# Column tiles for the scores and the state products of a linear-attention and mixture-of-experts kernel, with re-chosen priorities

## The chip, the cores and the metric

The kernel runs on one core of a Trainium2 chip. The metric is the device time of one execution in microseconds (us). The core has a matrix engine (TensorE: PE in the rows for matmuls, PEld for its weight loads), a vector engine (VectorE, DVE), a scalar engine (ScalarE, ACT), GpSimd (POOL) and a queue engine (SP), and 16 DMA engines that move data between main memory and the on-chip memories. Every engine works through its own instructions in the order in which the program lists them.

## The reference

Three layers follow each other. The first is a linear attention with a complex decay, over 4 batches, 8 heads, 768 steps and a head size of 48:

```python
for t in range(S):
    ar, ai = a_re_n[:, :, t, :, None], a_im_n[:, :, t, :, None]   # normalised to a length of at most 0.999
    new_re = ar * S_re - ai * S_im
    new_im = ar * S_im + ai * S_re
    kv = np.einsum('bhd,bhe->bhde', k[:, :, t], v[:, :, t])
    S_re, S_im = (new_re + kv, new_im)
    y[:, :, t] = np.einsum('bhd,bhde->bhe', q[:, :, t], S_re)
```

The second layer is dense: `h = x @ w_in`, `g = max(h, 0) + alpha * min(h, 0)`, `x = g @ w_out`, with 3072 tokens, 384 features and 2048 hidden units. The third sends each token whose skip score is positive to one of 8 experts (the largest gate logit), each with 384 x 1024 and 1024 x 384 weights, and adds the gated result to the token.

## The kernel before

**Attention in chunks.** The 768 steps are cut into 6 chunks of 128 steps, and chunk and batch together give 24 steps `s`. For each `s`, `elementwise(s)` (labels `E0` to `E23`) turns the decays into running products and phases on ScalarE and VectorE and writes scaled queries `qh` and keys `kh`, 96 rows (real and imaginary part) by 8 heads by 128 steps. `attention(s)` (labels `P0` to `P23`) then does, on TensorE:

- scores (parts `a` and `b`, one for each group of 4 heads): for each head a product of `kh` and `qh` into the PSUM tile `at`, 128 by 128, key steps in the rows and query steps in the columns. One VectorE instruction multiplies all four by a triangular mask into the tile `A`.
- transposed keys: 4 transposes into another `at`, then one ScalarE copy into `kT`. The last chunk, s = 20 to 23, has none, and no state product either.
- outputs (part `y`): `columns(ops)` lists small products with 32 columns of weights each, so that four of them stand side by side in the 128 columns of the array. 16 use the values `vt` as weights and `A` as moving data; from the second chunk on 16 more use the state `St` and `qh`.
- state (part `s`): for each head one product of `kT` (96 columns of weights) and `vt` (48 moving columns) into `sps`, then VectorE updates `St`.

A float32 product is two weight loads and two matmuls in the trace.

**Dense layer.** `moe_block(m)` (labels `M0` to `M11`) takes 256 tokens, that is, two steps `s`. Each value is split into a high and a low part, so each product is three matmuls: into `h` with 256 moving columns, into `acc` with 394. The weights are decoded at the beginning from 64-bit words (labels `d0` to `d15`).

**Experts.** From about 556 us on, `start_of(n)` reads the place of each of 9 items into SP's registers, `gather` fetches an item's tokens by an indirect DMA into `xg`, `load_weights` fetches its weights, and `item` does its products and scatters the result. `gates_of` computes the gate from `xg` on VectorE.

**Order.** The order of all instructions on all engines is made ahead by a planner (`Plan`). Each operation has an engine, an estimated cost, what it depends on, and a priority. The planner plays these costs through and takes, on each engine, the ready operation with the lowest priority number; the order that comes out is the program. Priorities are made from the step number plus a table of single corrections, `SHIFT`, by label and part. For a DMA `lag` and `late` give the time that it takes. What the planner assumes only shapes the order; on the chip an engine waits for what its next instruction really needs.

```python
def start_of(n):                                        # in the planner 0.2 us on SP
    return pl.add("SP", 0.2, read, [plan], [])
pl.add("POOL", 1.1, go, [ids], [xg[:, t, :]], lag=0.7, late=1.0)   # a gather
pl.add("PE", 0.3 + 0.0575 * len(ops), go, ...)          # columns(ops)
```

While the weights are decoded (27 to 55 us in the plan) the planner puts extra matmuls where TensorE would idle.

The line numbers in the profile are those of helpers: L462 is every plain matmul, L467 a transpose, L731 the products of `columns`, L431 a two-tensor operation on VectorE, L439 a scalar-tensor-tensor operation, L424 a ScalarE copy, L419 an activation, L1002 and L1003 the register loads of `start_of`, L1046 the fetch of an item's list, L1056 a gather, L1014 an expert's weights.

Of the kernel before, what the change touches and what calls it, by code (L numbers as in the profile page):

```python
# [11 lines left out]
F32 = mybir.dt.float32  # L12
# [386 lines left out]
def moe_kernel(tc, a, qk, v, w_in, w_out, alpha, w_gs, w1, w2, nat, nat_v, out):  # L399
# [53 lines left out]
    def mm(o, l, r, start, stop):  # L453
        n = cols(o)
        dt = l.dtype
        if dt == F32R:
            cost = max(n, 256) / 2.4 + 13.5
        elif dt == BF16:
            cost = 30
        else:  # L460
            cost = 2 * (max(n, math.prod(l.shape[1:])) / 1.2 + (6 if n <= 128 else 0))
# [31 lines left out]
    with ctx:  # L493
# [12 lines left out]
        mask = cp.tile([128, 128], BF16, name="mask")  # L506
        nc.gpsimd.memset(mask, 1.0)
        nc.gpsimd.affine_select(out=mask, in_=mask, pattern=[[1, 128]], compare_op=ALU.is_ge,
                                fill=0.0, base=0, channel_multiplier=-1)
# [60 lines left out]
        for x in qhs:  # L570
            nc.gpsimd.memset(x.ap()[96:128, :, :], 0.0)
        dec = ExitStack()
# [93 lines left out]
        def attention(s, pri):  # L666
# [12 lines left out]
            m4 = mask.rearrange("p (o f) -> p o f", o=1).to_broadcast([128, 4, 128])  # L679
            As, kTs = [], []  # L680
            for g in range(2):
                pl.pri, pl.part = pri(g), 'ab'[g]
                at = pbuf(at_ps, [128, 512], "at", bufs=2)
                for x in range(4):
                    mm(at[:, x * 128:(x + 1) * 128], kh[:, 4 * g + x, 0:128], qh[0:96, 4 * g + x, :], True, True)
                A = pl.buf(pp, [128, 4, 128], F32, "A", bufs=2)
                tt(A, at.rearrange("p (x t) -> p x t", x=4), m4, ALU.mult)
                As.append(A)
                if not last:
# [4 lines left out]
                    copy(kT, at[:, 0:384].rearrange("p (x d) -> p x d", x=4))  # L694
# [11 lines left out]
            columns(ops)  # L706
            pl.pri, pl.part = pri(3), 's'
            if not last:
                sps = pbuf(s_ps, [128, H * D], "sps")[0:96, :]
                for h in range(H):  # L710
                    mm(sps[:, h * D:h * D + D], kTs[h // 4][:, h % 4, :], vt[:, h * 64:h * 64 + D], True, True)
# [12 lines left out]
            tt(xlo[:, :, cs], y, xhi[:, :, cs], ALU.subtract)  # L724
            pl.part = ''

        def columns(ops):

            def go():
                for n, (o, l, r) in enumerate(ops):  # L730
# [821 lines left out]
```

## Time and profile before

| | us |
|---|---|
| median of 3 runs | 762.5 (762.09 to 762.78) |
| the profiled execution, its own time | 760.46 |
| its span, first to last instruction | 758.3 |
| TensorE busy in the span | 718.6 |
| VectorE busy | 602.1 |
| ScalarE busy | 486.7 |

The times are read as device time of one execution. The span is what the trace covers; the profiled execution's time is 2.2 us longer than its span and 2.0 us under the median. Busy time of TensorE is the union of modelled durations that overlap, so it tells where the engine stood still and not how much work there was; the work is better read from start to start.

### The profile page before, as it was taken

Reading aid. Unit: us, or ns where it says so; the run is one execution under the profiler, and the core shown is the slowest. Engines: PE = TensorE matmul, PEld = TensorE weight load, DVE = VectorE, ACT = ScalarE, POOL = GpSimd, SP = SyncE. Lnnn points to the kernel's source line nnn. Section 1 sums busy time; section 2 is a strip of 40 time slices with the busy share of each in tenths; the row PEclk is TensorE's granted clock in tenths of the full one; section 3 lists DMA queues with packets and bytes.
Section 4 is the critical chain, followed back from the end, with each engine's and each line's share of the span. In section 5 each row is a group of like instructions: output and inputs, shape, how many; then the busy total and the mean of one; then the engine's idle time right before and its main releaser. Section 6 shows DMA issues by size and latency. Waiting matters only on the chain.

```text
span 758.3 us, 16570 instructions
## 1 busy us (share of the span) xinstructions
PE 718.6 (95%) x6372; PEld 695.5 (92%) x6372; DVE 602.1 (79%) x1425; ACT 486.7 (64%) x833; POOL 98.6 (13%) x154
## 2 busy tenths in 40 slices
PE   1789999999999999999999999999997999999996
PEld 0678999999999999999999999999997999999996
DVE  5999999989889899999899898945555635697623
ACT  8969659869779679897948958522325332556411
POOL 4000000111101220011130010101011013710111
PEclk9999999999999999999999999999999999999999
DMA  7595862483744767668475564936215301899500
GB/s 267 161 273 199 239 214 79 124 257 102 189 117 143 188 175 231 183 181 268 137 195 178 180 193 120 250 108 172 87 44 189 126 1 46 274 390 393 181 11 18
DMA packets 84678, 130.53 MB, mean 172 GB/s; under 512 B 8822, under 2 KB 60096, under 8 KB 84592
## 3 DMA queue, kind: packets, MB, share of 16 engines
q1 hardware_dynamic: 79152, 111.19, 48.4%
q0 software_dynamic: 5440, 18.21, 7.6%
q8 instruction: 52, 0.85, 0.5%
q14 instruction: 34, 0.28, 0.1%
HBM read 99.46 MB, written 31.29 MB: 172 GB/s over the span
## 4 chain that ended last, share of the span: by engine, by line
PE 49%; issue 10%; DVE 7%; ACT 5%; DMA 5%; SPq 2%; POOL 1%; POOLq 0%; ACTq 0%; DVEq 0%
PE h L462 20%; PE acc L462 19%; PE at L462 3%; PE y L731 3%; PE sps L462 2%; ACT X L419 2%; ACT L391 2%; DVE X L431 1%; DMA r<-in_w 1%; DMA qh<-qd 1%; PE at L467 1%; DMA lst<-tok,ix 1%; DMA X<-in_qk 1%; DMA kd<-QP 1%; ACT hs L424 1%
## 5 line engine op out<-in xcount | busy, mean ns | idle before, releaser
L462 PE MATMUL h<-xlo,wih 128*128 128x256 f32 x576 | 163.8, 285 | 0.2 <-DVE xlo L431 0.2
L462 PE MATMUL h<-xhi,wih 128*128 128x256 f32 x576 | 162.9, 289 | 0.7 <-ACT hs L424 0.4
L462 PE MATMUL h<-xhi,wil 128*128 128x256 f32 x576 | 163.0, 284 | 0.0
L462 PE MATMUL acc<-woh,gh 128*128 128x394 f32 x384 | 134.4, 350 | 0.2 <-ACT gh L424 0.2
L462 PE MATMUL acc<-woh,gl 128*128 128x394 f32 x384 | 130.4, 347 | 4.2 <-DVE gl L431 4.2
L462 PE MATMUL acc<-wol,gh 128*128 128x394 f32 x384 | 132.1, 344 | 0.0
L419 ACT ACTIVATE X<-X 128x384 f32<-128x384 f32 (+1 forms) x216 | 117.2, 559 | 20.9 <-DVE X L450 7.0
L462 PEld LDWEIGHTS h<-xhi,wih 128*128 128x128 f32 x576 | 108.6, 190 | 3.1 <-ACT hs L424 1.3
L462 PEld LDWEIGHTS h<-xlo,wih 128*128 128x128 f32 x576 | 109.7, 191 | 0.7 <-DVE xlo L431 0.4
L462 PEld LDWEIGHTS h<-xhi,wil 128*128 128x128 f32 x576 | 109.7, 191 | 0.4 <-issue 0.4
L439 DVE SCALAR_TENSOR_TENSOR hs<-hs,alp 128x256 f32<-128x256 f32 x192 | 83.8, 477 | 28.6 <-ACT hs L424 28.1
L424 ACT COPY hs<-h 128x512 f32<-128x512 f32 x96 | 53.7, 583 | 63.0 <-PE h L462 60.7
L391 ACT ACT_TABLE_LOAD x71 | 91.1, 1283 | 1.1
L424 ACT CAST gh<-hs 128x512 fp32r<-128x512 f32 x96 | 58.4, 616 | 47.7 <-DVE hs L439 25.0
L431 DVE TENSOR_TENSOR gl<-hs,gh 128x512 fp32r<-128x512 f32 x96 | 65.2, 685 | 14.8 <-ACT gh L424 14.6
L462 PEld LDWEIGHTS acc<-woh,gl 128*128 128x128 f32 x384 | 71.6, 190 | 5.8 <-DVE gl L431 4.7
L911 POOL DMA_INDIRECT lst<-tok,ix x24 | 36.2, 1510 | 312.1 <-DVE ix L435 261.5
L431 DVE TENSOR_TENSOR X<-X 128x768 f32<-128x768 f32 (+1 forms) x96 | 71.6, 749 | 5.8 <-ACT X L419 5.6
L462 PEld LDWEIGHTS acc<-woh,gh 128*128 128x128 f32 x384 | 72.9, 190 | 1.5 <-ACT gh L424 0.6
L462 PEld LDWEIGHTS acc<-wol,gh 128*128 128x128 f32 x384 | 73.1, 190 | 0.3 <-issue 0.2
L462 PE MATMUL at<-qh,kh 96*128 96x128 f32 x384 | 52.6, 278 | 1.0 <-DMA qh<-qd 1.0
L439 DVE SCALAR_TENSOR_TENSOR X<-X 128x384 f32<-128x384 f32 x96 | 52.1, 549 | 0.9 <-ACT X L419 0.6
(189 smaller groups left out, 1381.1 us busy)
## 6 DMA issues: line engine op xcount, KB each, us to landing
r<-in_w SPq DMA_DIRECT2D x24, 512.0 KB, 7.2
r<-in_w SPq DMA_DIRECT2D x32, 384.0 KB, 8.9
kd<-QP SPq DMA_DIRECT2D x24, 387.0 KB, 4.9
kh<-kd SPq DMA_DIRECT2D x24, 387.0 KB, 4.7
qd<-X SPq DMA_DIRECT2D x24, 384.0 KB, 4.0
qh<-qd SPq DMA_DIRECT2D x24, 384.0 KB, 4.5
X<-in_a POOLq DMA_DIRECT2D x18, 384.0 KB, 5.6
X<-in_qk POOLq DMA_DIRECT2D x18, 384.0 KB, 6.1
```

What stands on the lines that cost most here:

```text
L391: nc.scalar.preload_act_table_set(o)
L419: lambda: nc.scalar.activation(real(o), real(i), f, **{k: real(x) for k, x in kw.items()}),
L424: lambda: nc.scalar.copy(real(o), real(i)), [i], [o])
L431: dve(o, cols(o), lambda: nc.vector.tensor_tensor(out=real(o), in0=real(x), in1=real(y), op=op), [x, y], late=late)
L439: dve(o, cols(o), lambda: nc.vector.scalar_tensor_tensor(out=real(o), in0=real(x), scalar=real(s), in1=real(y), op0=op0, op1=op1), [x, y, s])
L462: pl.add("PE", cost / 1e3, lambda: nc.tensor.matmul(real(o), lhsT=real(l), rhs=real(r), start=start, stop=stop, skip_group_check=True), [l ...
L467: pl.add("PE", 0.09 if cols(o) <= 96 else 0.12, lambda: nc.tensor.transpose(real(o), real(i), ident), [i], [o])
L731: ins = nc.tensor.matmul(real(o), lhsT=real(l), rhs=real(r), start=n < 4, stop=n >= len(ops) - 4, skip_group_check=True)
L911: r = nc.gpsimd.indirect_dma_start(out=lst, out_offset=bass.IndirectOffsetOnAxis(ap=real(ix[:, t:t + 1].bitcast(U32)), axis=0), in_=toks[t ...
```

## The change

The scores of a head become two column tiles of 64 rows. The first has the first 64 key steps as weights and all 128 query steps as moving data; the second has the last 64 key steps and only the last 64 query steps, since the quarter with later keys and earlier queries is masked to zero anyway. For odd heads the two halves of the key steps change places in the array, so that each half of the array has as many columns to stream. `A` is now one of two fixed tiles, cleared once at the start, and the mask is applied by three VectorE instructions in place of one: one of 256 columns on 128 rows, two of 128 columns on 64 rows. Since the key steps of odd heads are swapped, the copy into `kT` becomes three ScalarE copies (even heads; odd heads, each half of the rows to the other half), and the values are swapped in the same way on the host.

The state product of a head becomes three column tiles of 32 weight columns, all heads in one call of `columns`. `columns` has two new arguments: whether each product stands alone, and the planner's cost.

Every entry of `SHIFT` is new. Some costs in the planner change: a matmul of more than 256 columns 2.5 ns more, the two register loads of `start_of` 1.0 us in place of 0.2, the landing of a gather 1 us later. On GpSimd the old mask goes and two masks and two cleared tiles come at the start.

```diff
 SHIFT = {
-    "E0e": 1.5, "E1e": 5.5, "E2e": 3, "E2k": 3.5, "E2x": 2, "E3e": 1.6, "E3k": 4, "E4e": 5.1, "E4q": 2.7,
...
+    "E0k": -60.1, "E2e": -8.5, "E2q": -5.6, "E3e": -16.4, "E3q": -0.5, "E4e": -6.3, "E4q": -8.2, "E5e": -7,
...
-            cost = max(n, 256) / 2.4 + 13.5
+            cost = max(n, 256) / 2.4 + (13.5 if n <= 256 else 16)
...
-        mask = cp.tile([128, 128], BF16, name="mask")
...
+        near = cp.tile([128, 2, 64], BF16, name="near")
...
+        late = cp.tile([128, 4, 64], BF16, name="late")
...
+        A2 = [keep(sp, [128, 4, 128], F32, f"A{n}") for n in range(2)]
+        for x in A2:
+            nc.gpsimd.memset(x.ap(), 0.0)
...
                 at = pbuf(at_ps, [128, 512], "at", bufs=2)
+                ops = []
                 for x in range(4):
-                    mm(at[:, x * 128:(x + 1) * 128], kh[:, 4 * g + x, 0:128], qh[0:96, 4 * g + x, :], True, True)
-                A = pl.buf(pp, [128, 4, 128], F32, "A", bufs=2)
-                tt(A, at.rearrange("p (x t) -> p x t", x=4), m4, ALU.mult)
+                    qx, kx = qh[0:96, 4 * g + x, :], kh[:, 4 * g + x, :]
+                    lo, hi = (0, 64) if x % 2 == 0 else (64, 0)
+                    ops.append((at[lo:lo + 64, x * 128:(x + 1) * 128], kx[:, 0:64], qx))
+                    ops.append((at[hi:hi + 64, x * 128 + 64:(x + 1) * 128], kx[:, 64:128], qx[:, 64:128]))
+                columns(ops, True, 0.1 + 4 * 0.17)
+                A = A2[g]
+                at4 = at.rearrange("p (x t) -> p x t", x=4)
+                tt(A[:, :, 64:128], at4[:, :, 64:128], late, ALU.mult)
+                for half in range(2):
+                    ps = slice(64 * half, 64 * half + 64)
+                    tt(A[ps, half:4:2, 0:64], at4[ps, half:4:2, 0:64], near[ps, half, :].rearrange("p (o t) -> p o t", o=1).to_broadcast([64, 2, 64]), ALU.mult)
...
-                    copy(kT, at[:, 0:384].rearrange("p (x d) -> p x d", x=4))
+                    a4 = at[:, 0:384].rearrange("p (x d) -> p x d", x=4)
+                    copy(kT[:, 0:4:2, :], a4[:, 0:4:2, :])
+                    copy(kT[64:128, 1:4:2, :], a4[0:64, 1:4:2, :])
+                    copy(kT[0:64, 1:4:2, :], a4[64:128, 1:4:2, :])
...
-            columns(ops)
+            columns(ops, False, 0.3 + 0.0575 * len(ops))
...
-                for h in range(H):
-                    mm(sps[:, h * D:h * D + D], kTs[h // 4][:, h % 4, :], vt[:, h * 64:h * 64 + D], True, True)
+                columns([(sps[j:j + 32, h * D:h * D + D], kTs[h // 4][:, h % 4, j:j + 32], vt[:, h * 64:h * 64 + D])
+                         for h in range(H) for j in (0, 32, 64)], True, 0.3 + H * 0.09)
...
-            return pl.add("SP", 0.2, read, [plan], [])
+            return pl.add("SP", 1.0, read, [plan], [])
...
-                pl.add("POOL", 1.1, go, [ids], [xg[:, t, :]], lag=0.7, late=1.0)
+                pl.add("POOL", 1.1, go, [ids], [xg[:, t, :]], lag=0.7, late=2.0)
...
+    vv[:, :, 1::2] = np.roll(vv[:, :, 1::2], 64, axis=1)
```

## Rows read from the trace of the kernel before

**Rows 1.** The page: span, and busy time of each engine.

```profile
span 758.3 us, 16570 instructions
PE 718.6 (95%) x6372; PEld 695.5 (92%) x6372; DVE 602.1 (79%) x1425; ACT 486.7 (64%) x833; POOL 98.6 (13%) x154
```

**Rows 2.** Waits of TensorE: engine, line, releaser; us in total, times, longest.

```profile
PE at L467 <- DVE Ao L439: 19.8, 3, 15.4
```

**Rows 3.** Windows: length, busy PE, PEld, DVE, ACT, POOL, clock, DMA share, GB/s.

```profile
75.00:550.00 475.00, 472.53 (x4474) 458.51 (x4474) 419.21 (x995) 340.69 (x583) 49.70 (x54) 1.00 0.60 173
...
275.00:300.00 25.00, 25.00 (x235) 24.75 (x236) 24.98 (x54) 20.10 (x35) 5.03 (x4) 1.00 0.79 229
```

**Rows 4.** Timeline of TensorE's matmuls from 300 us: start, us, instructions merged.

```profile
300.15 1.05 PE L462 MATMUL at<-qh,kh 96*128 96x128 f32 x8
301.04 0.49 PE L467 MATMUL at<-ident,kh 96*128 96x96 f32 x4
301.37 0.80 PE L462 MATMUL sps<-vt,kT 128*96 128x48 f32 x8
301.99 0.48 PE L462 MATMUL h<-xhi,wih 128*128 128x256 f32 x2
302.31 0.28 PE L462 MATMUL h<-xlo,wih 128*128 128x256 f32 x1
302.43 0.28 PE L462 MATMUL h<-xhi,wil 128*128 128x256 f32 x1
```

**Rows 5.** The same timeline around one step's outputs, from 556 us.

```profile
556.67 0.28 PE L462 MATMUL h<-xhi,wil 128*128 128x256 f32 x1
556.88 1.08 PE L731 MATMUL y<-qh,St 128*32 128x128 f32 x32
557.77 1.06 PE L731 MATMUL y<-A,vt 128*32 128x128 f32 x32
558.76 0.39 PE L462 MATMUL h<-xhi,wih 128*128 128x256 f32 x1
558.99 0.28 PE L462 MATMUL h<-xlo,wih 128*128 128x256 f32 x1
```

**Rows 6.** Tiles sps and y: durations min/median/max in ns, first and last start.

```profile
L462 PEld LDWEIGHTS sps<-vt,kT x320: 159/165/166, 42.2 to 484.0; 128*96 128x96 f32 x160
...
L731 PEld LDWEIGHTS y<-A,vt x768: 106/110/110, 44.6 to 558.5; 128*32 128x32 f32 x192
```

**Rows 7.** Windows, tile y alone: instructions under way in a tenth of a microsecond.

```profile
304.42:304.53 0.11, 0.10 (x4) 0.10 (x8) 0.00 (x0) 0.00 (x0) 1.00 1.16 223
```

**Rows 8.** Groups by line and shape on DVE and ACT: busy us, mean ns.

```profile
L431 DVE TENSOR_TENSOR A<-at,mask 128x512 f32<-128x512 f32 x48 | 32.7, 683 | 5.1 <-PE at L462 4.1 <-PE y L731 0.7
...
L431 DVE TENSOR_TENSOR xlo<-y,xhi 128x384 fp32r<-128x384 f32 x24 | 13.2, 551 | 3.4 <-ACT xhi L424 3.3
...
L424 ACT COPY kT<-at 128x384 f32<-128x384 f32 x40 | 18.9, 473 | 10.7 <-PE at L467 10.7
```

**Rows 9.** Timelines of VectorE from 307 us.

```profile
307.88 0.55 DVE L431 TENSOR_TENSOR xlo<-y,xhi 128x384 fp32r<-128x384 f32 x1
308.35 0.68 DVE L431 TENSOR_TENSOR A<-at,mask 128x512 f32<-128x512 f32 x1
```

**Rows 10.** Source line L1002, then timelines of SP, POOL, DVE and PE, 556 to 579 us.

```profile
L1002 SPq TENSOR_LOAD <-plan x9: 263/263/469, 556.0 to 565.2; - x9
...
566.97 0.42 SPq L1046 DMA_DIRECT2D ids<-lst  x1
...
571.10 1.02 POOL L1056 DMA_INDIRECT xg<-x1d,ids  x1 [0.30 <-issue]
...
577.44 0.17 DVE L446 TENSOR_REDUCE gmx<-xg 128x2 f32<-128x16 f32 x1 [8.24 <-issue]
...
578.48 0.70 PE L462 MATMUL acc<-woh,gl 128*128 128x394 f32 x1 [3.98 <-DVE gl L431]
```

**Rows 11.** Windows after that wait and later, columns as in the windows above.

```profile
578.30:581.70 3.40, 3.22 (x10) 3.23 (x11) 3.29 (x10) 2.09 (x4) 0.00 (x0) 0.50 0.12 42
```

More of the change, by code (lines that the diff above doesn't have):

```diff
@@ L505, in moe_kernel @@
         make_identity(nc, ident)
-        mask = cp.tile([128, 128], BF16, name="mask")
-        nc.gpsimd.memset(mask, 1.0)
-        nc.gpsimd.affine_select(out=mask, in_=mask, pattern=[[1, 128]], compare_op=ALU.is_ge,
-                                fill=0.0, base=0, channel_multiplier=-1)
+        near = cp.tile([128, 2, 64], BF16, name="near")
+        nc.gpsimd.memset(near, 1.0)
+        for half in range(2):
+            nc.gpsimd.affine_select(out=near[:, half, :], in_=near[:, half, :], pattern=[[1, 64]], compare_op=ALU.is_ge,
+                                    fill=0.0, base=64 * half, channel_multiplier=-1)
+        late = cp.tile([128, 4, 64], BF16, name="late")
+        nc.gpsimd.memset(late, 1.0)
+        for x in range(4):
+            if x % 2 == 0:
+                nc.gpsimd.affine_select(out=late[:, x, :], in_=late[:, x, :], pattern=[[1, 64]], compare_op=ALU.is_ge,
+                                        fill=0.0, base=64, channel_multiplier=-1)
+            else:
+                nc.gpsimd.affine_select(out=late[0:64, x, :], in_=late[0:64, x, :], pattern=[[1, 64]],
+                                        compare_op=ALU.is_ge, fill=0.0, base=0, channel_multiplier=-1)
         one = cp.tile([128, 1], F32, name="one")
@@ L678, in attention @@
             y = pbuf(y_ps, [128, 3, 128], "y")
-            m4 = mask.rearrange("p (o f) -> p o f", o=1).to_broadcast([128, 4, 128])
             As, kTs = [], []
@@ L683, in attention @@
                 at = pbuf(at_ps, [128, 512], "at", bufs=2)
+                ops = []
                 for x in range(4):
-                    mm(at[:, x * 128:(x + 1) * 128], kh[:, 4 * g + x, 0:128], qh[0:96, 4 * g + x, :], True, True)
-                A = pl.buf(pp, [128, 4, 128], F32, "A", bufs=2)
-                tt(A, at.rearrange("p (x t) -> p x t", x=4), m4, ALU.mult)
+                    qx, kx = qh[0:96, 4 * g + x, :], kh[:, 4 * g + x, :]
[6 more added lines that the diff above has]
+                tt(A[:, :, 64:128], at4[:, :, 64:128], late, ALU.mult)
+                for half in range(2):
+                    ps = slice(64 * half, 64 * half + 64)
+                    tt(A[ps, half:4:2, 0:64], at4[ps, half:4:2, 0:64], near[ps, half, :].rearrange("p (o t) -> p o t", o=1).to_broadcast([64, 2, 64]), ALU.mult)
                 As.append(A)
@@ L725, in attention, with columns @@
             pl.part = ''
-        def columns(ops):
+        def columns(ops, alone, cost):
             def go():
                 for n, (o, l, r) in enumerate(ops):
-                    ins = nc.tensor.matmul(real(o), lhsT=real(l), rhs=real(r), start=n < 4,
-                                           stop=n >= len(ops) - 4, skip_group_check=True)
+                    ins = nc.tensor.matmul(real(o), lhsT=real(l), rhs=real(r), start=alone or n < 4,
+                                           stop=alone or n >= len(ops) - 4, skip_group_check=True)
                 return ins
-            pl.add("PE", 0.3 + 0.0575 * len(ops), go, [x for op in ops for x in op[1:]], [op[0] for op in ops])
+            pl.add("PE", cost, go, [x for op in ops for x in op[1:]], [op[0] for op in ops])
         def decode64(src, n, name):
```

54 rows, old and new, of the table SHIFT are left out of this document.

## The prediction

> **What bounds the kernel now.** I read the page first: TensorE is busy 719 of 758 us, VectorE 602, ScalarE 487 [rows 1]. Busy time of TensorE overlaps, so the second view is who waited: its one long wait ahead of 75 us is for VectorE's decoding, 19.8 us in three times [rows 2]. The windows then show TensorE without a hole from 75 to 550 us, 472.5 of 475 us, with VectorE busy 419 and ScalarE 341 [rows 3]. So from 75 us on, a microsecond of TensorE work less is a microsecond less, if VectorE follows. It has 56 us to spare in those 475, but not everywhere: from 275 to 300 us it is busy 24.98 of 25.
>
> The work itself is read from start to start in the timeline. Eight score matmuls take 301.04 - 300.15 = 0.89 us, 0.111 each; eight state matmuls take 301.99 - 301.37 = 0.62, 0.078 each; an `h` matmul takes 0.12, but the first two behind the state matmuls take 0.32 in place of 0.24 [rows 4]. The outputs already run in column tiles: 32 matmuls take 557.77 - 556.88 = 0.89 us, so a set of four tiles, 128 moving columns each, takes 0.111, as long as one matmul that fills the array [rows 4, 5].
>
> Changing to column tiles and back has a price. From the end of the `h` matmul before (556.67 + 0.12) to the second one after, less 0.12 for the first (558.99 - 0.12), the outputs take 2.08 us; their 16 sets are 1.78. The borders cost 0.30 [rows 5].
>
> One hole stands behind 550 us. SP reads the places of nine items from 556.0 to about 566 us, more than 1.1 us each where the planner counts 0.2; only then does it fetch the first list (567.0), and the gather is issued at 571.1. The gate of the first item waits for it on VectorE, which does its work in order: 8.24 us idle until 577.44. The `gl` behind it comes late, and TensorE stands 3.98 us [rows 10]. Afterwards the granted clock is half for 3.4 us, 1.2 in place of 2.4 GHz [rows 11], which costs another 1.7.
>
> **State products** (20 steps). Removed: 16 matmuls, 16 x 0.078 + 0.08 at the border = 1.33 us. Added: 48 matmuls in 16 sets of three tiles with 48 moving columns. No row has such a set. By the outputs' rate, 0.111 x 48 / 128 = 0.042, so 0.67, and with borders as for the outputs (0.30) 0.97. That gains 0.36 a step, 7.2 us. Bad end: a set is no faster than one state matmul now, 1.25 + 0.30 = 1.55, a loss of 0.22 a step, 4.4 us. Good end: every one stands beside outputs, with the same tiles, and pays no border: 0.66 a step, 13 us. I take 7.2, since the streamed columns set the outputs' pace.
>
> **Scores** (48 groups). Removed: 0.89 us. Added: 16 matmuls on two halves of the array. Two heads put 128 + 64 columns, twice, on each half: 384 x 0.111 / 128 = 0.33, so a group takes 0.67. Borders: between nothing (gain 0.22, 10.6 us in all) and the outputs' 0.30 (0.97: a loss of 0.08, 3.8 us). No row shows a border of two tiles, and the border of plain products costs 0.08 when `h` follows but none when the transposes follow [rows 4], as they do here; I take the middle, 0.15, a gain of 0.07, 3.4 us.
>
> Both together are 10.6 us. The outputs run from 44.6 to 558.5 us [rows 6], 24 steps, so one or two lie ahead of 75 us, where TensorE isn't the bound. I count two out, 22/24: 9.7 us.
>
> **A rule against it.** In the outputs a weight load of 32 columns is recorded with 110 ns, one of 96 columns with 165, so a column costs 0.86 ns and 32 columns 0.027 us [rows 6]; the outputs' set of 0.111 holds a stream of 128 columns and shows no 0.027 on top, and eight loads are under way in a window of 0.11 us with four matmuls [rows 5, 7]. The Trainium skill, page "TensorE: Matmul & The Clock Gate", section "Part 3: Packing small matmuls", says that a weight load overlaps with running matmuls only if its row group differs, which column tiles of the same rows don't have. By that rule a set of the outputs would take 0.138; the trace disagrees. By the row the sum is the 9.7 above; by the rule it is the last rival below.
>
> **Mask and transposed keys.** VectorE's mask of 512 columns takes 683 ns, 384 columns 551: 1.03 ns a column and 155 fixed [rows 8]. So 256 columns take 419 and 128 columns 287, and the three instructions 993 in place of 683: 0.31 more. Start to start an instruction of 0.55 takes 0.47, so 0.08 of each lies under the next [rows 9], and the increase is 0.15. Over 48 groups 7 to 15 us, in 75 to 550 us some 6.6 to 13.6. The cover is VectorE's 56 us of idle there; in stretches like 275 to 300 there is none, and there TensorE may wait. I take 1 us, bounds 0 and 13.6. On ScalarE one copy of 473 ns becomes three of half and a quarter the size; each at most 473, so at most 0.95 more, 40 times 38 us [rows 8], beside 134 idle [rows 3]. It costs nothing there, but the state product waits for both copies; TensorE has `h` and `acc` matmuls to do meanwhile. If that cover is gone, up to 0.95 a group shows.
>
> **Start.** GpSimd clears two tiles and makes two masks more; it is busy 99 us of 758 [rows 1], and the first outputs come at 44.6 us [rows 6]. Nothing; as a bound 1 us.
>
> **Costs and priorities.** With 1.0 for a read the planner's nine reads last 9 us in place of 1.8, close to the 10 in the trace, and the gather lands 1 us later in its plan. So it knows the first gate to be ready 8 us later than it thought, and VectorE gets other work ahead of it. What remains is the gap to the real landing, and TensorE went on for 5 us after VectorE stood still (569.2 to 574.5), so a wait of 3 or 4 us wouldn't reach it. I count the 3.98 + 1.7 = 5.7 us as gained; bounds 0 and 5.7. The other priorities are numbers whose effect no row shows: at best they close the 2.5 us of 475 that TensorE doesn't work, at worst they make another hole of 5.7. I take 0.
>
> **Sum.** 9.7 + 5.7 - 1 = 14.4 us less: the profiled execution 746 in place of 760.5. The median of the runs is 2.0 above the profiled execution; from 762.5 this is 748.
>
> **Rivals.**
> *The hole stays.* The first gate still stands too early in VectorE's order, since SP issues the weights' transfers ahead of the gather, and these hold it back. Gain 9.7 - 1 = 8.7: 754. For it: the gather's delay is mostly behind other transfers and the plan knows only 1 us more of it. Against: 8 us is as long as VectorE stood.
> *VectorE becomes the bound.* It decides once the added 6.6 to 13.6 us fall where VectorE has no idle time. 762.5 - 9.7 + 6.6 to 13.6, with the hole kept or closed: 754 to 766. For it: 24.98 of 25 us. Against: on the mean 419 + 13.6 = 433 in the 465 that remain.
> *Weight loads go one after the other,* however many tiles. The outputs don't exclude it by their pace: four loads of 0.027 are 0.11 as well. Then the scores' 16 loads of 64 columns take 16 x 0.055 = 0.88 + 0.15, 0.14 more than now, 6.7 us; the state's 48 take 1.32 + 0.30, 0.29 more, 5.8 us. 22/24 of that is 11.5 slower: with the hole closed 768, with it 774. It decides if the state's set takes over 0.064 (1.33 less 0.30, over 16). Against it: eight loads within 0.11 us, where in turn there would be four [rows 7].
> *A load doesn't hide behind its own tile's matmul.* Then a state set takes 0.027 + 0.042 = 0.069, 1.40 a step, 1.4 us slower in all; a pair of heads takes 0.33 + 4 x 0.055 = 0.55, a group 1.25, 0.36 more, 17 us slower; 779 with the hole. This is what the skill's rule above would make; by rows 5 it is nearly excluded.
>
> **How the numbers follow.** Chances: forecast 0.42, hole stays 0.22, VectorE bound 0.15, loads in turn 0.10, loads not hidden 0.02, clearly better than forecast (both products near their good ends) 0.05, a worse order for reasons no row shows 0.04. This kernel's measurement tells 0.2%, 1.5 us, from no change. Faster: the first two, the better case and two thirds of VectorE's, 0.79; same: a fifth of VectorE's and a little of the last, 0.04; slower: 0.17. The forecast's own range is 742 to 753. The range that should hold 8 in 10 reaches down to half of the way to the good ends ((13 - 7.2) / 2 + (10.6 - 3.4) / 2 = 6.5, to 741) and up to the end of VectorE's case, 766; outside are the loads' rivals, some of the last and the clearly better case.
>
> **What would show it.** In the trace after: sets of three state matmuls about 0.045 apart and the whole some 0.7 us; a group of scores in 0.7 us from first to last start; the first matmul behind each phase late by 0.1 or 0.2; VectorE's three mask instructions at 420 and 290 ns; no wait of TensorE near 570 us and no clock of 0.5 behind it. Wrong would make it: sets of scores that aren't side by side, since the two matmuls of a float32 product follow each other on one tile; holes of TensorE over 1 us between 100 and 500 us that VectorE ends; a new hole where the experts begin.

## The result and the profile after

The changed kernel takes 773.14 us (769.68 to 777.29, 4 runs) against 762.3 (761.82 to 762.78, 4 runs) for the kernel before on the same chip: a ratio of 1.0149 (1.011 to 1.0188), slower. Forecast were 748.0 and a range of 741 to 766. The profiled execution took 772.7 us.

The page of the changed kernel answers to [rows 1]:

```profile
span 770.9 us, 18807 instructions
...
PE 719.1 (93%) x7400; PEld 678.0 (88%) x7400; DVE 618.7 (80%) x1521; ACT 507.0 (66%) x911; POOL 98.8 (13%) x162
```

TensorE is as busy as before (719.1 against 718.6 us) in a span that is 12.6 us longer. The windows, columns as in [rows 3], show that it is no longer without a hole:

```profile
75.00:550.00 475.00, 459.91 (x5245) 426.77 (x5248) 428.77 (x1065) 354.93 (x651) 45.51 (x54) 0.99 0.60 171
275.00:300.00 25.00, 24.13 (x281) 22.35 (x282) 22.78 (x61) 20.55 (x40) 4.73 (x6) 1.00 0.66 197
...
65.00:69.00 4.00, 3.92 (x20) 3.92 (x21) 3.50 (x10) 3.07 (x6) 0.00 (x0) 0.57 0.46 164
92.00:100.00 8.00, 7.53 (x28) 6.92 (x29) 5.96 (x14) 4.16 (x10) 1.07 (x2) 0.57 1.02 341
119.00:124.00 5.00, 4.65 (x33) 4.33 (x33) 4.26 (x11) 4.04 (x10) 0.00 (x0) 0.66 0.55 163
```

Not busy are 15.1 us of 475, where it was 2.5; weight loading fell from 458.5 to 426.8. Between 275 and 300 us VectorE was busy 24.98 of 25 us and is now busy 22.78: it waits more too. The last three rows are stretches in which the granted clock was mostly at its lower level, 1.2 GHz; in the kernel before it was 1.00 from 75 to 550 us [rows 3]. Of 4, 8 and 5 us at 0.57, 0.57 and 0.66, some 13.7 us are at half the clock, which costs up to 6.8 us; in the kernel before, the 3.4 us behind the hole [rows 11] cost up to 1.7. Both also end with 4 to 5 us at half clock. So up to 5 of the 12.2 us by which the two profiled executions differ go through the clock. They are not the whole: the fastest execution of the changed kernel took 769.68 us at a mean granted clock of 0.996, the same as that of the profiled execution before, which took 760.46. The waits of TensorE, columns as in [rows 2], hold no single cause:

```profile
PE at L475 <- DVE Ao L447: 20.6, 3, 15.5
PE at L470 <- ACT wt L432: 6.6, 5, 3.4
PE h L470 <- ACT hs L432: 3.4, 4, 1.3
PE at L763 <- DVE A L439: 2.8, 4, 1.2
...
PE acc L470 <- ACT gh L432: 1.3, 3, 0.5
PE sps L763 <- ACT kT L432: 1.3, 2, 0.8
```

The first row is the wait at the beginning that was there before (19.8), and most of the second, on decoded weights, lies ahead of 75 us too. Behind them come a few waits each on ScalarE's and VectorE's part of the dense layer (`hs`, `gh`), on the mask (`A`) and on the copies (`kT`); from 75 to 550 us none of TensorE's waits is longer than 1.7 us. A matmul of `h` is recorded with 0.28 us while the next starts 0.12 later [rows 4], so a gap of up to 0.16 us between two of them doesn't show as idle time at all.

The products themselves, in the timeline of TensorE around one group of scores and one step's state, answer to [rows 4]:

```profile
304.84 0.34 PE L470 MATMUL acc<-woh,gl 128*128 128x394 f32 x1
305.11 0.89 PE L763 MATMUL at<-qh,kh 96*64 96x128 f32 x16
305.93 0.55 PE L475 MATMUL at<-ident,kh 96*128 96x96 f32 x4
306.26 0.36 PE L470 MATMUL h<-xhi,wih 128*128 128x256 f32 x1
306.46 0.28 PE L470 MATMUL h<-xlo,wih 128*128 128x256 f32 x1
...
308.36 0.28 PE L470 MATMUL h<-xhi,wil 128*128 128x256 f32 x1
308.57 0.88 PE L763 MATMUL sps<-vt,kT 128*32 128x48 f32 x48
309.39 0.63 PE L470 MATMUL acc<-woh,gl 128*128 128x394 f32 x2
309.85 0.34 PE L470 MATMUL acc<-woh,gh 128*128 128x394 f32 x1
```

The tiles do run side by side. The 48 state matmuls are recorded as 0.88 us from the start of the first to the end of the last; one lasts 0.206, so their starts span 0.67, and the 15 steps between 16 sets are 0.045 each. With the borders (from the last product before, plus its usual spacing of 0.12 or 0.18, to the second product behind, less its spacing) a state product of 16 sets takes 1.00 us in the undisturbed places, against 1.39 before. A group of scores with its four transposes, measured in the same way, takes 1.326 us in place of 1.248: the 16 matmuls start within 0.66, but the first stands 0.09 late (305.11 against 304.84 + 0.18) and the transposes 0.16 behind the last. The second `h` behind the transposes comes 0.20 after the first in both kernels, where 0.12 is usual.

The groups by line and shape answer to [rows 8]:

```profile
L439 DVE TENSOR_TENSOR A<-at,near 64x128 f32<-64x128 f32 x96 | 27.3, 284 | 1.0
...
L439 DVE TENSOR_TENSOR A<-at,late 128x256 f32<-128x256 f32 x48 | 20.1, 419 | 5.4 <-PE at L763 4.4 <-PE y L763 0.6
...
L432 ACT COPY kT<-at 64x192 f32<-64x192 f32 x80 | 25.1, 313 | 2.1 <-PE at L475 0.7
...
L432 ACT COPY kT<-at 128x192 f32<-128x192 f32 x40 | 12.6, 315 | 14.5 <-PE at L475 14.1
```

The masks take 419 + 2 x 284 = 987 ns in place of 683, 14.7 us in all; the copies 315 + 2 x 313 = 941 ns in place of 473, 18.8 us in all.

Where the experts begin, the rows that answer to [rows 10] are these, from the source line of the reads, SP and GpSimd:

```profile
L1034 SPq TENSOR_LOAD <-plan x9: 260/267/462, 578.4 to 588.9; - x9
...
582.72 0.42 SPq L1078 DMA_DIRECT2D ids<-lst  x1
...
585.48 1.06 POOL L1088 DMA_INDIRECT xg<-x1d,ids  x1 [5.71 <-DMA ids<-lst]
```

The list is fetched 4.3 us after the first read (before: 11.0), and TensorE has no wait that the view of waits would list between 550 and 640 us. The hole is closed, as forecast, and still the kernel is slower.

### The profile page after: what moved, and what is told of

Same layout as the page of the kernel before. It is cut to its first block, busy times and chain, and to the rows that moved or that the text cites. A ratio compares the mean times of both kernels' runs of the same rounds, so it can differ in the third digit from the quotient of the medians.

```text
span 770.9 us, 18807 instructions
## 1 busy us (share of the span) xinstructions
PE 719.1 (93%) x7400; PEld 678.0 (88%) x7400; DVE 618.7 (80%) x1521; ACT 507.0 (66%) x911; POOL 98.8 (13%) x162
## 4 chain that ended last, share of the span: by engine, by line
PE 35%; DVE 19%; ACT 17%; DMA 14%; issue 12%; POOL 2%; SPq 1%; POOLq 0%; ACTq 0%; DVEq 0%
PE acc L470 15%; PE h L470 12%; ACT X L427 6%; DMA r<-in_w 5%; DVE X L439 4%; ACT L399 3%; DVE hs L447 3%; PE at L763 2%; ACT Rr L427 2%; DVE X L447 2%; DVE gl L439 2%; PE y L763 2%; ACT kT L432 2%; DVE X L458 2%; ACT hs L432 1%
## 5 line engine op out<-in xcount | busy, mean ns | idle before, releaser
L470 PE MATMUL h<-xhi,wih 128*128 128x256 f32 x576 | 165.7, 293 | 6.5 <-ACT hs L432 3.4
L470 PEld LDWEIGHTS h<-xhi,wih 128*128 128x128 f32 x576 | 110.2, 193 | 12.6 <-ACT hs L432 6.2
L432 ACT COPY hs<-h 128x512 f32<-128x512 f32 x96 | 53.8, 583 | 50.2 <-PE h L470 44.1
L439 DVE TENSOR_TENSOR X<-X 128x384 f32<-128x384 f32 (+1 forms) x96 | 71.8, 750 | 10.8 <-ACT X L427 10.4
L439 DVE TENSOR_TENSOR gl<-hs,gh 128x512 fp32r<-128x512 f32 x96 | 65.2, 685 | 15.2 <-ACT gh L432 14.7
L943 POOL DMA_INDIRECT lst<-tok,ix x24 | 31.6, 1318 | 235.8 <-DVE ix L443 193.6
L479 POOL DMA_DIRECT2D X<-in_a x18 | 10.0, 556 | 338.7 <-DVE gl L439 100.1
```

Source lines behind the costliest of these rows:

```text
L432: lambda: nc.scalar.copy(real(o), real(i)), [i], [o])
L439: dve(o, cols(o), lambda: nc.vector.tensor_tensor(out=real(o), in0=real(x), in1=real(y), op=op), [x, y], late=late)
L470: pl.add("PE", cost / 1e3, lambda: nc.tensor.matmul(real(o), lhsT=real(l), rhs=real(r), start=start, stop=stop, skip_group_check=True), [l ...
L479: return pl.add(eng, 0.55 if eng == "SP" else 0.8, lambda: q.dma_start(real(o), real(i)), [i], [o], after, lag=took[0], late=took[1] - 0.5)
L943: r = nc.gpsimd.indirect_dma_start(out=lst, out_offset=bass.IndirectOffsetOnAxis(ap=real(ix[:, t:t + 1].bitcast(U32)), axis=0), in_=toks[t ...
```

## Experiments

The kernel before took 761.4 to 770.2 us on the chips that the experiments ran on, so each result is a ratio to its time on the same chip, with the 95% interval. "Old order" means that the planner works with the old operations, costs and priorities, and only the instructions that it places are exchanged; "new order" the reverse.

**New instructions or new order?**

The first kernel has the old order and all new instructions; of its edit, what stands in the place of four scores:

```diff
-mm(at[:, x * 128:(x + 1) * 128], kh[:, 4 * g + x, 0:128], qh[0:96, 4 * g + x, :], True, True)
+for o, l, r in ((at[lo:lo + 64, x * 128:(x + 1) * 128], kx[:, 0:64], qx),
+                (at[hi:hi + 64, x * 128 + 64:(x + 1) * 128], kx[:, 64:128], qx[:, 64:128])):
+    ins = nc.tensor.matmul(real(o), lhsT=l, rhs=r, start=True, stop=True, skip_group_check=True)
```

> The new instructions of the attention (score tiles, three masks, three copies, state tiles) put in place of the old ones in the old kernel's order; the planner still plans with the old costs and priorities, so every other instruction keeps its place, and the hole near 574 us may stay. From the phases in the changed kernel's trace: scores 0.07 to 0.12 us dearer a group, state 0.38 cheaper a step, so about 3 us less TensorE work. Theory order (the new order loses the time): 757 to 761 us, no waits of TensorE from 150 to 500 us beyond those of before. Theory instructions (the added VectorE and ScalarE instructions starve TensorE): 768 us or more.

Measured: 1.027 (1.0232 to 1.0309), as the theory of instructions had it.

The second has the new order and the old instructions; of its edit, one mask in the place of three:

```diff
+together(pl.ops[-3:], at.buf, 3, lambda A=A, at4=at4: nc.vector.tensor_tensor(
+    out=real(A), in0=real(at4), in1=m4, op=ALU.mult))
```

> The reverse: the changed kernel's order, planned with its costs and priorities, but the old instructions at the places of the new ones (one mask, one copy, plain score and state products). Theory order: still slow, 768 to 780 us, with the first dense block late by 10 us as in the changed kernel. Theory instructions: 755 to 762 us, since the hole near 574 us is closed and the added work gone.

Measured: 0.9995 (0.9974 to 1.0017). The new order by itself costs nothing and gains nothing; the new instructions cost 2.7% in the old order, and the new order gives 1.2% of that back.

**The state products alone**

```diff
+for j in (0, 32, 64):
+    ins = nc.tensor.matmul(o[j:j + 32, h * D:h * D + D], lhsT=k[h // 4][:, h % 4, j:j + 32],
+                           rhs=w[:, h * 64:h * 64 + D], start=True, stop=True, skip_group_check=True)
```

> Only the state products as three column tiles, in the old order. No added VectorE or ScalarE work. By the phases in the changed kernel's trace 0.38 us less on 18 of 20 steps: 7 us, so 755 us by both theories; 762 if TensorE isn't the bound after all.

Measured: 0.9996 (0.998 to 1.0012). Both theories had expected a gain; what came is the third case, 762, that of a TensorE that isn't the bound. Each state product takes 1.00 us here too, so 7.6 us of TensorE work are gone, but not from the time. The window from 275 us, columns as above, in the kernel before and in this one:

```profile
275.00:325.00 50.00, 50.00 (x534) 48.87 (x535) 49.61 (x105) 41.96 (x69) 7.16 (x8) 1.00 0.70 204
...
275.00:325.00 50.00, 48.71 (x633) 47.06 (x632) 49.81 (x109) 42.34 (x68) 7.87 (x8) 1.00 0.70 205
```

TensorE, without a hole there before, now idles 1.3 us, and VectorE is as full as it was: 49.8 of 50 us.

**Masks and copies**

The old order with three masks and three copies, and nothing swapped:

```diff
+nc.vector.tensor_tensor(out=a[:, :, 64:128], in0=p4[:, :, 64:128], in1=m4[:, :, 64:128], op=ALU.mult)
+for half in range(2):
+    ps = slice(64 * half, 64 * half + 64)
+    ins = nc.vector.tensor_tensor(out=a[ps, 2 * half:2 * half + 2, 0:64], in0=p4[ps, 2 * half:2 * half + 2, 0:64],
+                                  in1=m4[ps, 0:2, 0:64], op=ALU.mult)
...
+nc.scalar.copy(k[:, 0:4:2, :], a4[:, 0:4:2, :])
+nc.scalar.copy(k[64:128, 1:4:2, :], a4[64:128, 1:4:2, :])
+return nc.scalar.copy(k[0:64, 1:4:2, :], a4[0:64, 1:4:2, :])
```

> Only the added VectorE and ScalarE instructions in the old order: the mask in three instructions of the same sizes, the copy in three (not swapped, so a fourth of the masked scores is left at zero or unmasked data of the wrong quarter and the output isn't the reference's). TensorE's work is the old one. Theory order: 762 to 765 us. Theory instructions: 770 us or more.

Measured: 1.0208 (1.0182 to 1.0233). Most of the loss is here, with TensorE's instructions untouched. The next two kernels have one half of this edit each.

> Only the mask in three VectorE instructions, in the old order (a quarter of the masked scores stays zero, so the output isn't the reference's); TensorE and ScalarE as before. Both added parts together cost 16 us. Theory VectorE (it alone sets the pace): 772 to 777 us. Theory ScalarE: 761 to 764 us. Theory coupling (each engine's added time counts, since the three wait for each other in a fixed order): 767 to 771 us, in the ratio of the added times.

Measured: 1.0181 (1.0158 to 1.0204), some 14 us, as much as the masks' own 14.6 us. By its size this is what the theory of VectorE alone asked for (772 to 777 us against 762).

> Only the transposed keys in three ScalarE copies, in the old order (same result as one copy); TensorE and VectorE as before. Theory VectorE: 761 to 764 us. Theory ScalarE: 772 to 777 us. Theory coupling: 766 to 770 us.

Measured: 1.0104 (1.0087 to 1.0121), some 8 us of the 19 that the copies add on ScalarE. That is the theory of coupling; by the theory of VectorE alone the copies cost nothing. Alone the two halves cost 2.9% together, in one kernel 2.1%, so a part of the two overlaps. The waits of TensorE in the kernel with the masks, between 125 and 520 us:

```profile
PE h L462 <- ACT hs L424: 1.8, 5, 0.6
PE at L462 <- DMA qh<-qd: 1.3, 2, 0.9
PE acc L462 <- ACT gh L424: 1.2, 3, 0.7
...
PE sps L462 <- ACT kT L424: 0.7, 1, 0.7
...
PE at L462 <- DVE A L711: 0.6, 1, 0.6
```

Only one wait names the mask. The others are for results that pass through VectorE or ScalarE behind it. With TensorE's order the same, each matmul can be compared with its own start before: the delay is 3.7 us at 173, 7.3 at 278, 11.0 at 378, 14.4 at 482 us and 15.9 at 595, so it grows while attention runs and then hardly any more. Of the 10.7 us from 173 to 482, over 27 groups, some 1.3 us are one stop at 437 us that the kernel without the reductions, further down, shows on the same chip as well; the rest is about 0.35 us a group.

**Is VectorE full?**

```diff
 red(chk[:, s:s + 1], W[:, 1, :], ALU.min)
+pl.ops[-1].fn = lambda: None
```

> Less VectorE work in the old order: the 80 reductions that check the inputs (0.54 us each, 0.46 from start to start, 37 us in all) are left out and their results set to passing values; the transfers stay. For these inputs the output doesn't change. Theory VectorE or coupling (TensorE only looks busy): 735 to 752 us. Theory TensorE (it is the bound and only added work hurts): 759 to 762 us.

Measured: 0.9981 (0.9959 to 1.0003). The window from 275 us, where VectorE was fullest:

```profile
275.00:325.00 50.00, 50.00 (x535) 48.87 (x534) 45.24 (x94) 41.94 (x69) 6.88 (x8) 1.00 0.69 203
```

VectorE has 4.8 us of idle in 50 and TensorE doesn't move. The control is work added in other places:

```diff
+nc.vector.tensor_reduce(out=scrap, in_=real(i), axis=AX.X, op=ALU.min)
 return fn()
```

> The kernel before, with one more reduction of 144 columns (about 0.30 us) ahead of each of the 80 reductions that check the inputs; its result is thrown away. That adds about 24 us to VectorE between 100 and 542 us, more than the three masks add (14 us), in pieces of the same size, and nothing on TensorE waits for it directly. Theory that only added time in the chain from scores to outputs counts: ratio 1.000 to 1.006 (up to 5 us, where a reduction has mask work right behind it). Rival, any work added to VectorE counts: as for the masks, 24/14 of 1.8%, so 1.025 to 1.035.

Measured: 1.011 (1.0089 to 1.013), between the two. A microsecond added in the reductions costs a third of a microsecond, one added in the masks a whole one: the place counts, but work off the chain isn't free either. Then the other direction:

```diff
-tt(A, at.rearrange("p (x t) -> p x t", x=4), m4, ALU.mult)
+nc.vector.tensor_tensor(out=a[:, :, 64:128], in0=p4[:, :, 64:128], in1=m4[:, :, 64:128], op=ALU.mult)
```

> The kernel before, but each of the 48 masks covers only the later 64 query steps of each head (256 of 512 columns, in one instruction); the other half of the tile stays zero, so the outputs of the earlier 64 steps lack their share from within the chunk. A mask takes about 0.42 us in place of 0.68. That takes 12.6 us from VectorE; leaving 43 us of reductions out gave nothing. Theory that the mask lies in the chain that sets the pace: about as much back as the longer masks cost, 0.985 to 0.992 (6 to 11 us less). Rival, the longer masks cost because they are more instructions, or because VectorE as a whole was near full: within 0.3% of the kernel before.

Measured: 0.9989 (0.9972 to 1.0006). The theory that the mask alone sets the pace missed: a longer mask costs, and of the 12.6 us of a shorter one hardly anything shows.

**Scores as tiles, state products whole**, with the edit of the first kernel, three masks and three copies, odd heads swapped:

```diff
+nc.scalar.copy(k[:, 0:4:2, :], a4[:, 0:4:2, :])
+nc.scalar.copy(k[64:128, 1:4:2, :], a4[0:64, 1:4:2, :])
+return nc.scalar.copy(k[0:64, 1:4:2, :], a4[64:128, 1:4:2, :])
```

> Scores as tiles of 64 rows with their masks in three and copies in three (odd heads swapped), in the order of the kernel before; the state products stay whole. With masks and copies in three alone the ratio was 1.021. Theory that the score tiles cost 0.07 to 0.12 us a group for their borders: 1.024 to 1.029. Rival, the tiles save 0.07 a group as forecast and the cost is masks and copies alone: 1.016 to 1.021.

Measured: 1.0295 (1.0265 to 1.0325). Against masks and copies alone that is 0.9% more. By the rows the tiles cost 0.078 us a group, 3.7 us or 0.5%. Much of the rest lies in the head of the profiled execution, where the clock is at half for some 10 us:

```profile
61.00:72.00 11.00, 11.00 (x90) 8.87 (x86) 7.33 (x21) 8.24 (x20) 0.00 (x0) 0.53 0.24 83
```

At 75 us its `h` matmuls are 6.2 us later than in the kernel before, with masks and copies alone 2.7. From 75 to 430 us the two fall behind by another 14.6 and 12.8 us. Whether the tiles make the clock fall there isn't shown.

**Two full engines, or a chain?** Four kernels put the edits above together with the reductions left out, in the old order but for the last:

```diff
 red(chk[:, 120 + n:121 + n], raw.bitcast(F32)[:, :, 1], ALU.min, True)
+pl.ops[-1].fn = lambda: None
```

> Order of before; state products as column tiles, and the 80 reductions that check the inputs left out, so TensorE has 7.6 us less and VectorE 43 us less; each alone gave 1.000 and 0.998. Theory of two limits (TensorE is full, VectorE right behind it): the saving of the state tiles appears, 0.988 to 0.993. Rival, the saving is lost in the waits from engine to engine, which no reduction touches: 0.997 to 1.000.

Measured: 0.9975 (0.9951 to 0.9998), in the rival's range. The trace shows that a part of the saving is there all the same. With each `h` and `acc` matmul held against its own start in the kernel before, this kernel gains 3.3 us from 75 to 430 us, of some 5.7 us that 15 state products save by then; the state tiles alone gain 0.5, the missing reductions alone 0.2. (The comparison ends at 430 us, since the stop at 437 us shows on some chips and not on others.)

> Order of before; masks in three instructions (one quarter of the masked scores stays zero, as in the run of the masks alone) and the 80 reductions left out, so VectorE has 14 us more and 43 us less. Theory of two limits: VectorE's work as a whole decides, and the ratio falls from 1.018 to 0.998 to 1.006. Rival, the chain scores, mask, outputs decides: it stays at 1.014 to 1.019.

Measured: 1.014 (1.0115 to 1.0164). Its window, columns as above:

```profile
75.00:550.00 475.00, 467.41 (x4415) 448.99 (x4415) 400.28 (x1000) 342.12 (x588) 46.86 (x54) 1.00 0.60 173
```

VectorE is busy 19 us less than in the kernel before [rows 3], and the masks still cost most of what they did by the ratio. Of the profiled execution's loss 5.8 us are there at 75 us already, behind two stretches with the clock at half:

```profile
49.00:57.00 8.00, 6.88 (x28) 5.76 (x29) 6.52 (x17) 3.50 (x8) 0.00 (x0) 0.57 0.77 221
70.00:74.00 4.00, 3.99 (x21) 4.00 (x22) 3.76 (x9) 2.46 (x5) 0.00 (x0) 0.57 0.89 273
```

From 75 to 430 us it loses 6.8 us more; the masks with the reductions lose 10.5 there. So by these two executions a third of the masks' cost goes with the room on VectorE, and two thirds stay.

> Order of before; copies of the transposed keys in three instructions on ScalarE and the 80 reductions left out. Alone the copies gave 1.010. Theory that the copies cost because VectorE, which needs ScalarE's results, has no slack to catch up: 0.998 to 1.003. Rival, ScalarE or the chain transposes, copy, state product decides by itself: it stays at 1.007 to 1.011.

Measured: 1.0118 (1.0089 to 1.0147): unchanged; from 75 to 430 us it loses 5.7 us, with the reductions 6.7.

> The changed kernel with its own order and without the 80 reductions; with them it had 1.015. Theory of two limits: VectorE's added 14 us are more than made up, and the ratio falls to 0.995 to 1.005. Rival, the cost lies in chains that no reduction touches: 1.010 to 1.016.

Measured: 1.0082 (1.0057 to 1.0107), between the two. So neither theory holds alone: room on VectorE gives back a third of the masks' cost, a little of the copies', half of the changed kernel's loss, and lets about half of the state tiles' saving appear; the larger part of masks and copies stays. A reading that fits what is left, argued and not shown, is a chain without slack: the order places each product just where its input is ready. A longer mask or copy then shows at once; a shorter one finds TensorE full; and less work on TensorE finds mask and copy not yet done. That asks for both together: state products as tiles and half masks, and in a second kernel half copies as well:

```diff
-copy(kT, at[:, 0:384].rearrange("p (x d) -> p x d", x=4))
+pl.ops[-1].fn = lambda kT=kT, at=at: nc.scalar.copy(
+    real(kT)[:, 0:2, :], real(at[:, 0:192]).rearrange("p (x d) -> p x d", x=2))
```

> Order of before; state products as column tiles, and each mask covers only the later 64 query steps of a head (the rest of the tile stays zero, so that share of the outputs is missing). Alone, the tiles gave 1.000 and the shorter masks 0.999. Theory of a chain without slack: together they give 0.990 to 0.996 (3 to 7.6 us). Rival, the saving of the tiles is lost in waits that the mask doesn't touch: 0.997 to 1.000.

Measured: 0.9965 (0.9939 to 0.9991), half a thousandth outside the expected 0.990 to 0.996, and its interval reaches into both theories. In its trace it gains 3.7 us from 75 to 430 us, hardly more than the state tiles with the reductions left out (3.3): whether VectorE's time is taken from the masks or elsewhere makes no difference that shows.

> The same, and the copy of the transposed keys takes only two of four heads (the others stay zero, so their states are missing), some 0.2 us shorter in each of 40 groups. Theory of a chain without slack: as much as or more than the kernel before it, 0.988 to 0.995. Rival, the waits are elsewhere: 0.997 to 1.000.

Measured: 0.9934 (0.9915 to 0.9953), in the range of the chain. State tiles, shorter masks: neither gives anything clear of noise alone (0.9996, 0.9989); together there are 3 us, with copies shorter too 5. What the copies add isn't shown: the two intervals overlap, this trace gains about 4.0 us from 75 to 430 us (2.3, and 1.7 for 3.4 us at the lower clock from 174 us on) where the other gained 3.7, and shorter copies alone weren't run.

**The better version: the new order, state tiles, and scores, masks and copies as before**

```diff
+pl.ops[-1].fn = whole
...
+together(pl.ops[-3:], at.buf, 3, lambda A=A, at4=at4: nc.vector.tensor_tensor(
+    out=real(A), in0=real(at4), in1=m4, op=ALU.mult))
...
+together(pl.ops[-3:], kT.buf, 3, lambda kT=kT, a4=a4: nc.scalar.copy(real(kT), real(a4)))
```

> The new order with the state tiles alone: plain scores, one mask, one copy at the places of the new ones. The new order with all old instructions ran at 760.9 us. If TensorE is the bound there, 7 us less, 754 us; if VectorE and ScalarE set the pace, 760 to 762 us, as in the old order.

Measured: 0.992 (0.9874 to 0.9965).

> The kernel with the new order and the state products as tiles, but the scores, masks and copies of before, once more, for a closer interval: it had 0.992 (0.9874 to 0.9965). Theory that the state tiles save 7.6 us on TensorE and the order lets them show: 0.990 to 0.995. Rival, that run was luck and the saving is lost as it was in the old order: 0.998 to 1.001.

Measured: 0.993 (0.9904 to 0.9957). It beats both kernels: 764.0 us where the kernel before took 769.6. In the new order the saving of the state tiles shows, 5.3 us of the 7.6 by 520 us in the first of the two kernels and 4.8 in the second, each matmul against its own start in the kernel with the old instructions and the same order.

## Why the prediction was wrong

**Where the time came from.** As a chain of ratios, from one kernel to the next: masks and copies in three +2.1%, scores as tiles +0.9% (1.0208 to 1.0295), state products as tiles -0.25% (to 1.027), the new order -1.2% (to 1.0149). Each difference carries some 0.4% of uncertainty of its own; the links aren't all from one chip, and in the profiled executions a part of the second link and up to 5 us of the whole go through the lower clock in the head. The three low stretches of the changed kernel stand at the same places in the same kernel without the reductions (0.57, 0.57 and 0.66 again), while the executions in the new order with plain scores, one mask and one copy (one with the state products whole, two with them as tiles) have a clock of 1.00 from 50 to 89 us. So the stretches come with the new scores, masks and copies in that order, which together cost 2.2% there (0.993 to 1.0149).

**What bounds the kernel: the step that failed.** The prediction read "without a hole, 472.5 of 475 us" as "a microsecond of TensorE work less is a microsecond less, if VectorE follows", and took VectorE's 56 us of idle as room to follow. TensorE was indeed busy without a hole, and shorter masks or 43 us of reductions less gave nothing clear of noise. But the condition "if VectorE follows" was judged by sums of busy time, and these don't decide it. Masks and copies in three, priced at 1 us together, cost 2.1% (16 us) with TensorE's own work unchanged, and in the old order 7.6 us of TensorE less gave nothing. That it is decided by whether masks and copies come in time where the written order has them is argued above, not shown.

**Masks: sized right, priced wrong.** Forecast were 420 and 290 ns and an increase of 0.31 us a group or less; it is 0.30. "I take 1 us, bounds 0 and 13.6": measured are 14 us, the far bound. The cover that the prediction named, VectorE's idle time, is mostly not where the masks are: with 43 us more of it 1.4% were left by the ratio and two thirds by the trace. The rival "VectorE becomes the bound" gave the right size of this term; its mechanism accounts for about a third of it.

**Copies: "It costs nothing there".** The row gave the bound, 0.95 a group, and the copies took 0.94; the 134 us of idle ScalarE were no cover. Alone they cost 8 us, and 9 without the reductions. The prediction named "up to 0.95 a group" as what shows if the `h` and `acc` matmuls are no cover; some 0.2 of it a group did.

**Scores: wrong sign.** The stream came out as forecast (0.67 forecast, 0.66 between first and last start). The border was taken as 0.15 with 0.30 as the bad end; the phase with its transposes became 0.078 longer, which is the bad end of "a loss of 0.08". The prediction took the middle because transposes behind plain products paid no border; tiles pay one of 0.09 ahead of them in any case, and their transposes don't follow at once.

**State products: right.** Forecast 1.33 to 0.97, measured 1.39 to 1.00, the gain 0.38 for 0.36. In the old order it is worth nothing, in the new one 0.7%.

**The rule.** The sets of three tiles start 0.045 apart, where a load hidden behind nothing would make them 0.069 apart; loads in turn, the other rival, needed more than 0.064. The rule of the Trainium skill (page "TensorE: Matmul & The Clock Gate", section "Part 3: Packing small matmuls"), that a load overlaps running matmuls only if its row group differs, is not borne out here, as the prediction judged from the outputs.

**The hole and the priorities.** The hole closed, in the new order with the old instructions too. That was forecast to bring 5.7 us; with the old instructions the new order is at 0.9995, so as much is lost elsewhere. One place is seen: in that kernel the granted clock from 100 to 125 us is 0.86 where it was 1.00. The first outputs, which the prediction let start at most 1 us late, start 2.3 us later than before (46.9 us, [rows 6]). The clearing on GpSimd need not be what shows there: kernels in the old order without it start theirs at 45.2 to 46.4 us, and one with it (state tiles and half masks) at 44.1. The other priorities were taken as 0. With the old instructions the whole new order, the closed hole included, is worth nothing; with the new ones 9 us, so there it gives some room to longer masks and copies. How much of the 9 us is the hole wasn't separated.

**Still open.** Whether the masks cost by their time or by being three instructions isn't settled: the shorter mask tests less time, not fewer instructions. Which single hand-over takes the 0.35 us of a group isn't either, since the waits are spread over `hs`, `gh`, `kT` and `A`, and a part is in gaps too short to show. The reductions, which should not matter to a chain, return half of the loss in the changed kernel and a third of the masks' cost, and cost 1.1% when they are longer, so room on VectorE counts too. Why the state tiles' saving shows in the new order and not in the old one isn't settled: from 275 to 325 us VectorE is busy 49.8 us in the old order with the tiles and 45.5 in the new, but with the reductions left out it is 45.6 in the old order as well, and only about half of the saving showed.

## What to carry to other kernels

When an order is written out for an engine that is never idle, price an added 0.3 us in what it waits for at its full length until a row shows the slack in front of that very instruction; the idle sum of the engine that does the work tells little about it. Less work on the full engine needn't pay in an order that was written for more of it, so try each half of an edit alone and in both orders: here, in the new order, the half with no extra instructions on other engines gains 0.7%, the whole loses 1.5%. A busy share made of overlapping records can stay near 97% while the engine runs short of work; the spacing of the starts tells it earlier.

## What the runs showed of the hardware

Three column tiles side by side take 48 moving columns in 0.045 us a set, and a change to column tiles and back costs about 0.3 us a phase: 1.00 less 16 sets of 0.045 for the state products, and as much for scores with transposes behind (1.326 less 0.67 for the stream and 0.36, the time of four transposes between `h` matmuls). A ScalarE copy of 64 rows by 192 columns takes 313 ns, as long as one of 128 rows (315): halving the rows saves nothing. In the head of the changed kernel the granted clock was mostly at the lower of its two levels from 65 to 69, 92 to 100 and 119 to 124 us, with TensorE recorded as busy 3.92 of 4.00, 7.53 of 8.00 and 4.65 of 5.00 us; in the 15 us ahead of the first of them, from 50 to 65 us, it had been busy 11.92, where the kernel before was busy 13.55 and kept its clock.
